# A filter table saved to DRAM in the order in which it is read back, and table work moved between engines

## The chip, the cores and the metric

The kernel runs on one core of one Trainium2 chip. The metric is the device time of one execution in microseconds (us). The core has a matrix engine (TensorE, PE; its weight loads are listed as PEld), VectorE (DVE), ScalarE (ACT), GpSimd (POOL) and an engine that only issues transfers (SyncE, SP). Each engine works through its own instructions in their order, and waits where one needs the result of another engine or of a transfer. Transfers issued by SP and by POOL are carried out by the same 16 DMA engines.

## The reference

The input x has 8 batches of 3008 rows and 256 channels. Along the rows it is filtered in the frequency domain, and then each row goes through a two-layer network with an exact GELU between the layers.

```python
X = np.fft.rfft(x, axis=1)                      # x: (8, 3008, 256)
F = (filt_r + 1j * filt_i)[None, :, :]          # filt_r, filt_i: (1505, 256)
y = np.fft.irfft(X * F, n=3008, axis=1)
x = y.reshape(8 * 3008, 256)
h = x @ w_in                                    # w_in: (256, 2048)
g = 0.5 * h * (1.0 + erf(h / sqrt(2)))
out = g @ w_out                                 # w_out: (2048, 256), out: (24064, 256)
```

## The kernel before

The row number is split as 3008 = 47 x 64, and so is the frequency. A transform is then two smaller ones, each a matrix product with a table of sines. Batch 0 is transformed in a head, before the network can start, by functions whose names begin with c. Batches 1 to 7 are transformed beside the network of the batch before them, in four steps s1 to s4. Between the steps the data is written to DRAM and read back in another order: R1 after s1, R2 after s3.

The network is a list of slots. A tile t has 512 rows of the output and 16 slots. In slot s = 16 t + j TensorE computes one 128-wide piece j of the first layer of tile t (mm1), on which ScalarE then does the GELU, and a sixteenth of the second layer of tile t - 1 (mm2, or mm2_seven). The transforms, tables and loads are hung on slots by put(slot, function, arguments); what is hung on a slot comes before the matrix products of that slot on each engine.

```python
for s in range((NT + 1) * 16):
    t, jc = s // 16, s % 16
    for f, a in at.pop(s, ()):
        f(*a)
    if t >= 1:
        (m.mm2_seven if t - 1 in seven else m.mm2)(t - 1, jc)
    if t < NT:
        m.mm1(t, jc)
```

mm1 writes to PSUM banks of kind h (three of them), the second layer to kind o (two), and the transforms mostly to kind f (three). mm2_seven does the second layer with seven products in place of eight (Strassen's scheme, for all tiles but the first and the last). It needs sums of pieces of the GELU's output, made on VectorE for each tile (sums_1, sums_2, sums_3, tiles s_sb and g_sb), and sums of pieces of w_out, made once (weight_sums, tile w_sums).

The filters lie in the tile F, with 128 rows. Rows 0 to 63 are loaded from the inputs: q = 0 is a frequency and q = 1 its mirror. In the head, rows 64 to 127 are a copy of rows 0 to 63. From batch 1 on the rows are wanted in another order, in which even and odd rows (the parity, par) stand apart. So F is saved to DRAM (Fd) and read back.

```python
def save_filters(self):
    self.Fd = self.dram.tile([64, 2, K1, 256], BF16, tag="Fd", name="Fd")
    self.nc.sync.dma_start(out=self.Fd, in_=self.F[0:64])

def load_filters_again(self, k0, k):
    for par in range(2):
        for r in range(2):
            for q in range(2):
                o = 64 * par + 32 * r + 16 * q
                self.nc.sync.dma_start(out=self.F[o:o + 16, :, k0:k0 + k, :],
                                       in_=self.Fd[32 * q + (par ^ q):32 * q + 32:2, :, k0:k0 + k, :])
```

K1 is 24. The second step, s2, multiplies by a table (T2p) and by F. Product p uses k = 2p and 2p + 1 of F:

```python
def s2(self, b, p):                             # p = 0 .. 11
    ps = self.bank("ps_s2")
    for i in range(2):
        k = 2 * p + i
        nc.tensor.matmul(ps[...], lhsT=self.T2p[:, k]..., rhs=self.st[b, "b", k // 6][:, k % 6, :], ...)
    w = self.st[b, "p", p] = self.pp.tile([128, 2, 512], BF16, tag="p12", name="p12")
    nc.vector.tensor_tensor(out=w, in0=ps.unsqueeze(1).to_broadcast([128, 2, 512]),
                            in1=self.F[:, :, 2 * p:2 * p + 2, :]..., op=ALU.mult)
```

Its other input, b_sb, is read from R1 by r1, in four pieces, and R1 is written by s1, in four groups c of four transfers. The tile a_sb between has three buffers, so that the fourth group waits for the writes of the first.

```python
def s1(self, b, c):
    a = self.pa.tile([128, 2, 4, 256], BF16, tag="a", name="a_sb")        # 3 buffers
    ps = [[self.bank("ps_s1", "h" if i == h == 0 else "f") for h in range(2)] for i in range(2)]
    ...                                                                   # 8 products
    for i in range(2):
        for h in range(2):
            self._evac(a[...], ps[i][h], "act" if h else False)           # ScalarE, or VectorE
    for r in range(2):
        for h in range(2):
            nc.sync.dma_start(out=o[:, w:w + 4, :], in_=a[64 * r:64 * r + 48, h])
```

Tables for batches 1 to 7 are made in the first slots: T2p (table_2_parities, GpSimd), U (table_u_pick on GpSimd, table_u on PE and ACT) and T4a (table_4_rows and weights_4 on GpSimd, table_4_factors on PE and ACT, and table_4_all, 24 operations on GpSimd). Loads of x and of the weights are issued by GpSimd, in its order.

```python
def weight_sums(self):
    w = self.w_out_sb.rearrange("p (i k) (n o) -> p k n i o", k=2, n=2)
    q, tt = self.w_sums, self.nc.gpsimd.tensor_tensor
    for o, a, b, op in ((q[:, 0], w[:, 0, 1], w[:, 0, 0], ALU.subtract), ...):    # four sums
        for i in range(0, 8, 2):
            tt(out=o[:, i:i + 2], in0=a[:, i:i + 2], in1=b[:, i:i + 2], op=op)
...
if b == 1:
    s1, n1, r1, s2, n2, group, r2, s4, n4 = 0, 4, 15, 25, 2.5, 12, 62, 70, 0.62
unit = lambda p: s2 + group * (p // 4) + int(n2 * (p % 4))    # the slot of product p
...
put(0, m.table_2_parities)
put(1, m.table_u_pick, g)
put(1, m.table_4_rows, g)
put(1, m.weights_4, g)
put(10, m.load_filters_again, 0, 8)
put(16, m.load_filters_again, 8, 16)
put(4, m.weight_sums)
put(12, m.table_4_factors, g)
put(14, m.table_u)
put(15, m.table_4_all, g)
```

The whole kernel:

Of the kernel before, what the change touches and what calls it, by code (L numbers as in the profile page):

```python
# [12 lines left out]
BF16 = mybir.dt.bfloat16  # L13
# [6 lines left out]
K1 = 24  # L20
# [10 lines left out]
class _Mix:  # L31
# [62 lines left out]
            for q, a in enumerate((direct, mirror)):  # L94
                nc.gpsimd.dma_start(out=self.F[32 * q:32 * q + 32, t, k0:k0 + k, :], in_=a)

    def save_filters(self):
        self.Fd = self.dram.tile([64, 2, K1, 256], BF16, tag="Fd", name="Fd")
        self.nc.sync.dma_start(out=self.Fd, in_=self.F[0:64])

    def load_filters_again(self, k0, k):

        for par in range(2):
            for r in range(2):
                for q in range(2):
                    o = 64 * par + 32 * r + 16 * q
                    self.nc.sync.dma_start(out=self.F[o:o + 16, :, k0:k0 + k, :],
                                           in_=self.Fd[32 * q + (par ^ q):32 * q + 32:2, :, k0:k0 + k, :])

    def dup_filters(self, eng, k0, k):  # L110
        for k in range(k0, k0 + k, 2):
# [263 lines left out]
    def s1(self, b, c):  # L375

        nc = self.nc
        if c == 0:
            self.st[b, "R1"] = self.dram.tile([NB, 48, 256], BF16, tag="R1", name="R1")
        a = self.pa.tile([128, 2, 4, 256], BF16, tag="a", name="a_sb")  # L380
        x = self.st[b, "x"]
# [4 lines that stand above are left out]
                    w = 8 * c + 4 * r + 2 * i  # L386
                    nc.tensor.matmul(ps[i][h][64 * r:64 * r + 64, :], lhsT=self.T1s[64 * h:64 * h + NA],  # L387
                                     rhs=x[64 * h:64 * h + NA, w:w + 2, :], start=True, stop=True)
        for i in range(2):
            for h in range(2):  # L390
                self._evac(a[:, h, 2 * i:2 * i + 2, :].rearrange("p a b -> p (a b)"), ps[i][h], "act" if h else False)
        o = self.st[b, "R1"].rearrange("n q c -> q n c")
        for r in range(2):
            for h in range(2):
                w = HB * h + 8 * c + 4 * r
                nc.sync.dma_start(out=o[:, w:w + 4, :], in_=a[64 * r:64 * r + 48, h])
# [209 lines left out]
    def weight_sums(self):  # L606

        w = self.w_out_sb.rearrange("p (i k) (n o) -> p k n i o", k=2, n=2)
        q, tt = self.w_sums, self.nc.gpsimd.tensor_tensor
        for o, a, b, op in ((q[:, 0], w[:, 0, 1], w[:, 0, 0], ALU.subtract), (q[:, 1], w[:, 1, 1], q[:, 0], ALU.add),  # L610
                            (q[:, 2], w[:, 1, 1], w[:, 0, 1], ALU.add), (q[:, 3], w[:, 1, 0], q[:, 1], ALU.subtract)):
            for i in range(0, 8, 2):
                tt(out=o[:, i:i + 2], in0=a[:, i:i + 2], in1=b[:, i:i + 2], op=op)

    def quarters(self, t):

# [77 lines left out]
def kernel(  # L694
# [9 lines left out]
    m = _Mix(ctx, tc, x, filt_r, filt_i, moe_w_in, moe_w_out, out)  # L704
# [4 lines left out]
    g = m.small  # L709
    wide = ctx.enter_context(ExitStack())  # L710
    m.psum(wide, w=(2, 1), m=(1, 1), n=(5, 1))
    act = "act"
# [30 lines left out]

    nc.gpsimd.memset(m.vt[:, :, 96, :], 0.0)
    m.dup_filters(nc.gpsimd, 4, 20)
    m.save_filters()


    m.table_2_sin(0)
# [31 lines left out]
    for q in range(1, 7):  # L781
        if q < 6:
            m.c2(2 * q)
            if q + 2 < 6:
                m.c1t(q + 2, (act,))
            if q != 3:
                m.warm_up(2)
            m.c2(2 * q + 1)
        if q < 6:
            m.c3(2 * q - 2)  # L790
            if q == 3:
                m.table_3(2)
                m.table_3_copy(2, True)
            else:
                m.warm_up(1)
        else:
            m.c3(10, 1)
            m.warm_up(1)
            m.c3(11, 1)
# [20 lines left out]
    def put(slot, f, *a):  # L820
        at.setdefault(slot, []).append((f, a))

    def first(b):
        return (b * S // TCH) * 16

    for b in range(1, B):
        hi = first(b)
        if b == 1:
            s1, n1, r1, s2, n2, group, r2, s4, n4 = 0, 4, 15, 25, 2.5, 12, 62, 70, 0.62
        else:  # L830
            s1, n1, r1, s2, n2, group, r2, s4, n4 = hi - 94, 3.7, hi - 80, hi - 71, 3.4, 14, hi - 25, hi - 17, 1
        unit = lambda p: s2 + group * (p // 4) + int(n2 * (p % 4))
        for u in range(16):
            put(s4 + int(u * n4), m.s4, b, u // 2, u % 2)
        for c in range(4):
            put(s1 + int(c * n1), m.s1, b, c)
            put(r1 if c < 3 else unit(3) + 1, m.r1, b, c)
            put(r2 if c < 3 else s4 + int(4 * n4) + 1, m.r2, b, c)
        for p in range(12):
            put(unit(p), m.s2, b, p)  # L840
            if p % 4 == 3:
                put(unit(p) + 3, m.s3, b, p // 4)
                put(unit(p) + 4, m.s3_out, b, p // 4, 1)
        if b + 1 < B:
            for i in range(8):
                put(unit(i + 2) if b > 1 else 25, m.load_next, b, i + 2, i // 2, i % 2)

    put(0, m.table_2_parities)
    put(1, m.table_u_pick, g)
    put(1, m.table_4_rows, g)  # L850
    put(1, m.weights_4, g)
    put(10, m.load_filters_again, 0, 8)
    put(16, m.load_filters_again, 8, 16)
    put(4, m.weight_sums)
    put(12, m.table_4_factors, g)
    put(14, m.table_u)
    put(15, m.table_4_all, g)
    seven = range(1, NT - 1)
    for t in seven:
        for i, s in enumerate((12, 13, 15, 17)):  # L860
# [4 lines left out]
    for s in range((NT + 1) * 16):  # L865
        t, jc = s // 16, s % 16
# [37 lines left out]
```

## Time and profile before

| what | value |
|---|---|
| time, median of 3 runs | 759.7 us (759.42 to 761.75) |
| span of the profiled execution | 758.5 us |
| TensorE busy | 741.2 us, 98% |
| VectorE busy | 581.4 us, 77% |
| ScalarE busy | 547.6 us, 72% |
| GpSimd busy | 111.6 us, 15% |
| reload of F, 8 transfers of 128 KB | 5.1 us from issue to landing (median) |
| reload of F, 8 transfers of 256 KB | 12.1 us from issue to landing (median) |

The page of a profile gives busy time by engine, the chain of work that ended last, and the costliest groups of instructions, named by the line of the kernel, the engine and the tiles as out<-in. A busy PE is not PE at its peak: products at half clock count as busy. Questions put to the trace give windows (the busy time of each engine in a stretch of time, its clock and what the DMA engines moved), waits (who waited for whom and how long) and a timeline. A wait for several things is put down to what came last by the profile, which is not always the true cause.

### The profile page before, as it was taken

Reading aid. Unit: us, or ns where it says so; the run is one execution under the profiler, and the core shown is the slowest. Engines: PE = TensorE matmul, PEld = TensorE weight load, DVE = VectorE, ACT = ScalarE, POOL = GpSimd, SP = SyncE. Lnnn points to the kernel's source line nnn. Section 1 sums busy time; section 2 is a strip of 40 time slices with the busy share of each in tenths; the row PEclk is TensorE's granted clock in tenths of the full one; section 3 lists DMA queues with packets and bytes.
Section 4 is the critical chain, followed back from the end, with each engine's and each line's share of the span. In section 5 each row is a group of like instructions: output and inputs, shape, how many; then the busy total and the mean of one; then the engine's idle time right before and its main releaser. Section 6 shows DMA issues by size and latency. Waiting matters only on the chain.

```text
span 758.5 us, 20181 instructions
## 1 busy us (share of the span) xinstructions
PE 741.2 (98%) x8388; PEld 519.3 (68%) x8388; DVE 581.4 (77%) x1043; ACT 547.6 (72%) x967; POOL 111.6 (15%) x207
## 2 busy tenths in 40 slices
PE   8988899999999999999999999999999999999998
PEld 4835567666777667666677666766677766777776
DVE  7935888799677986889777897779977799666562
ACT  7885567766787677867778667876678767777773
POOL 7969600021000210002000120001200000000000
PEclk9999999999999999999999999999999999999999
DMA  9999935555624745347525465254562432501011
GB/s 147 221 191 172 197 107 130 148 120 124 140 78 126 159 112 113 100 131 169 119 75 141 139 132 127 79 165 111 105 168 65 140 92 81 129 29 57 29 57 57
DMA packets 91500, 90.71 MB, mean 120 GB/s; under 512 B 7632, under 2 KB 78416, under 8 KB 91088
## 3 DMA queue, kind: packets, MB, share of 16 engines
q1 hardware_dynamic: 83024, 73.43, 36.2%
q0 software_dynamic: 8384, 16.00, 13.9%
q8 instruction: 65, 1.06, 0.6%
q14 instruction: 27, 0.22, 0.1%
HBM read 57.15 MB, written 48.23 MB: 139 GB/s over the span
## 4 chain that ended last, share of the span: by engine, by line
PE 85%; DVE 7%; DMA 4%; issue 1%; ACT 1%; POOL 0%; SPq 0%; DVEq 0%; ACTq 0%; POOLq 0%
PE ps_h L569 38%; PE ps_o L657 35%; PE ps_s L455 3%; PE ps_s L427 2%; DVE p L413 2%; DVE s_sb L627 2%; PE ps_s L410 2%; PE ps_s L387 2%; DMA b_sb<-R 2%; PE ps_o L596 1%; DMA R<-a_sb 1%; DMA x_sb<-in_x_dram 1%; PE ps_c L517 1%; ACT y_sb L295 1%; DVE ost L680 1%
## 5 line engine op out<-in xcount | busy, mean ns | idle before, releaser
L572 ACT ACTIVATE g_sb<-ps_h 128x512 f16<-128x512 f32 x752 | 448.2, 599 | 191.1 <-PE ps_h L569 188.7
L569 PE MATMUL ps_h<-y_sb,w_in_sb 128*128 128x512 bf16 (+3 forms) x1600 | 448.2, 368 | 1.3 <-ACT g_sb L572 0.8
L657 PEld LDWEIGHTS <-g_sb 128*128 128x128 f16 x2880 | 190.3, 98 | 81.7 <-issue 16.9
L657 PEld LDWEIGHTS <-s_sb 128*128 128x128 f16 x2160 | 147.3, 98 | 51.3 <-issue 3.3
L569 PEld LDWEIGHTS <-w_in_sb 128*128 128x128 bf16 x1600 | 125.2, 98 | 9.3 <-issue 3.6
L657 PE MATMUL ps_o<-w_sums,g_sb 128*128 128x128 f16 x1440 | 125.0, 219 | 2.2 <-DVE t_sb L673 1.5
L657 PE MATMUL ps_o<-w_sums,s_sb 128*128 128x128 f16 x1440 | 124.5, 219 | 0.0
L627 DVE TENSOR_TENSOR s_sb<-g_sb 128x1024 f16<-128x1024 f16 x180 | 121.4, 697 | 0.0
L413 DVE TENSOR_TENSOR p<-ps_s,F 128x1024 bf16<-128x1024 f32 x84 | 102.6, 1221 | 23.2 <-PE ps_s L410 15.8
L657 PE MATMUL ps_o<-w_out_sb,g_sb 128*128 128x128 f16 x1440 | 118.4, 219 | 0.4
L118 POOL COPY gate<-p 1x1 bf16<-1x1 bf16 x40 | 19.4, 484 | 415.3 <-DVE p L413 415.3
L633 DVE TENSOR_TENSOR g_sb<-s_sb,g_sb 128x1024 f16<-128x1024 f16 x90 | 62.3, 693 | 1.1
L657 PE MATMUL ps_o<-w_out_sb,s_sb 128*128 128x128 f16 x720 | 62.2, 219 | 0.0
L640 DVE TENSOR_TENSOR s_sb<-g_sb 128x1024 f16<-128x1024 f16 x90 | 61.5, 683 | 0.0
L299 DVE TENSOR_SCALAR y_sb<-ps_s 128x376 bf16<-128x376 f32 x56 | 30.6, 546 | 28.9 <-PE ps_s L455 28.9
L297 DVE CAST a_sb<-ps_s 128x512 bf16<-128x512 f32 x56 | 36.1, 686 | 18.6 <-PE ps_s L387 15.4
L455 PEld LDWEIGHTS <-d_sb 96*128 96x128 bf16 x448 | 31.2, 98 | 26.4 <-issue 1.9
L675 DVE TENSOR_TENSOR t_sb<-t_sb,ps_o 128x256 f32<-128x256 f32 x45 | 18.7, 416 | 38.5 <-PE ps_o L657 38.5
L672 DVE TENSOR_TENSOR ost<-t_sb,ps_o 128x256 f32<-128x256 f32 x45 | 18.9, 419 | 31.2 <-PE ps_o L657 31.2
L680 DVE TENSOR_TENSOR ost<-t_sb,ps_o 128x256 f32<-128x256 f32 x90 | 33.7, 416 | 6.8 <-PE ps_o L657 6.8
L455 PE MATMUL ps_s<-T4a,d_sb 96*128 96x94 bf16 x448 | 37.1, 206 | 1.0 <-DMA d_sb<-R 0.9
L410 PE MATMUL ps_s<-b_sb,T2p 128*128 128x256 bf16 x168 | 32.3, 274 | 2.1 <-DMA b_sb<-R 2.1
(149 smaller groups left out, 524.3 us busy)
## 6 DMA issues: line engine op xcount, KB each, us to landing
out_dram<-ost SPq DMA_DIRECT2D x93, 256.0 KB, 2.7
x_sb<-in_x_dram POOLq DMA_DIRECT2D x64, 188.0 KB, 3.6
R<-a_sb SPq DMA_DIRECT2D x112, 96.0 KB, 2.2
b_sb<-R SPq DMA_DIRECT2D x28, 384.0 KB, 4.4
R<-v_sb SPq DMA_DIRECT2D x84, 128.0 KB, 2.4
d_sb<-R SPq DMA_DIRECT2D x56, 192.0 KB, 3.9
F<-Fd SPq DMA_DIRECT2D x8, 256.0 KB, 12.1
Fd<-F SPq DMA_DIRECT2D x1, 1536.0 KB, 9.9
```

Source lines behind the costliest of these rows:

```text
L297: self.nc.vector.tensor_copy(out=out, in_=in_)
L299: self.nc.vector.tensor_scalar(out=out, in0=in_, scalar1=scale, scalar2=None, op0=ALU.mult)
L410: nc.tensor.matmul(ps[:, 256 * i:256 * i + 256], lhsT=self.T2p[:, k].rearrange("p a b c d -> p (a b c d)"), rhs=self.st[b, "b", k // 6][:, ...
L413: nc.vector.tensor_tensor(out=w, in0=ps.unsqueeze(1).to_broadcast([128, 2, 512]), in1=self.F[:, :, 2 * p:2 * p + 2, :].rearrange("p t a b ...
L455: nc.tensor.matmul(ps[:, 94 * i:94 * i + 94], lhsT=d[:, (grp % 2) * 4 + i, 128 * half:128 * half + 128], rhs=self.T4a[:, 4 * grp + i], sta ...
L569: nc.tensor.matmul(ps[:, o:o + n], lhsT=self.w_in_sb[:, dc, jc * 128:jc * 128 + 128], rhs=self.ring[:, dc, off:off + n], start=(dc == 0), ...
L572: nc.scalar.activation(out=self.st["g", t][:, jc, :], in_=ps, func=AF.Gelu)
L627: self.nc.vector.tensor_tensor(out=self.st["s", t][:, i:i + 2], in0=a, in1=b, op=ALU.subtract)
L633: self.nc.vector.tensor_tensor(out=a21[:, k], in0=self.st["s", t][:, k, 0], in1=a22[:, k], op=ALU.add)
L640: self.nc.vector.tensor_tensor(out=self.st["s4", t][:, k], in0=a12[:, k], in1=s2[:, k], op=ALU.subtract)
L657: nc.tensor.matmul(ps[:, (m + 1) % 2, sub, :], lhsT=a[:, i, 128 * sub:128 * sub + 128], rhs=b[:, i], start=i == 0, stop=i == 7)
L680: v(out=c(h, 1 - h), in0=tt, in1=p, op=ALU.add)
```

## The change

Its parts:

- The copy of the filters in DRAM is laid out in the order in which it is read back. It is written in two calls of four transfers each, and read back in transfers of 32 rows of one of the two filters, in place of 16 rows of both.
- The first third of it (k = 0 to 7) is read back in the head, before the transfers of R1, and not at slot 10. The rest stays near its slot (17 in place of 16).
- The sums of the weights are made by VectorE, in four operations, and not by GpSimd in 16, at slot 17 and not 4.
- In batch 1 one of the two evacuations of s1 on ScalarE goes to VectorE.
- The table work of batch 1 has other slots and another order on GpSimd, and s2, r2 and s4 of batch 1 begin three slots earlier, with s4 spread wider.

It is meant to have the inputs of batch 1 ready earlier, and to leave GpSimd free for the table T4a.

```diff
-    def save_filters(self):
-        self.Fd = self.dram.tile([64, 2, K1, 256], BF16, tag="Fd", name="Fd")
-        self.nc.sync.dma_start(out=self.Fd, in_=self.F[0:64])
+    def save_filters(self, k0, k):
+        if "Fd" not in self.st:
+            self.st["Fd"] = self.dram.tile([2, 2, 16, 2, K1, 256], BF16, tag="Fd", name="Fd")
+        for t in range(2):
+            for q in range(2):
+                o = self.st["Fd"][:, q, :, t, k0:k0 + k, :].rearrange("a i k c -> i a (k c)")
+                if q:
+                    o = o[:, ::-1]
+                self.nc.sync.dma_start(out=o, in_=self.F[32 * q:32 * q + 32, t, k0:k0 + k, :])
 
     def load_filters_again(self, k0, k):
-        for par in range(2):
-            for r in range(2):
-                for q in range(2):
-                    o = 64 * par + 32 * r + 16 * q
-                    self.nc.sync.dma_start(out=self.F[o:o + 16, :, k0:k0 + k, :],
-                                           in_=self.Fd[32 * q + (par ^ q):32 * q + 32:2, :, k0:k0 + k, :])
+        for t in range(2):
+            for o in range(0, 128, 32):
+                i = self.st["Fd"][o // 64, :, :, t, k0:k0 + k, :].rearrange("q i k c -> (q i) (k c)")
+                self.nc.sync.dma_start(out=self.F[o:o + 32, t, k0:k0 + k, :], in_=i)
@@ s1
-                self._evac(a[:, h, 2 * i:2 * i + 2, :]..., ps[i][h], "act" if h else False)
+                self._evac(a[:, h, 2 * i:2 * i + 2, :]..., ps[i][h], "act" if h and (b > 1 or i) else False)
@@ weight_sums
-        q, tt = self.w_sums, self.nc.gpsimd.tensor_tensor
+        q, tt = self.w_sums, self.nc.vector.tensor_tensor
-            for i in range(0, 8, 2):
-                tt(out=o[:, i:i + 2], in0=a[:, i:i + 2], in1=b[:, i:i + 2], op=op)
+            tt(out=o, in0=a, in1=b, op=op)
@@ the head
-    m.save_filters()
+    for k in (12, 0):
+        m.save_filters(k, 12)
@@ the head, q counts 1 to 6
             m.c3(2 * q - 2)
+            if q == 2:
+                m.load_filters_again(0, 8)
@@ batch 1
-            s1, n1, r1, s2, n2, group, r2, s4, n4 = 0, 4, 15, 25, 2.5, 12, 62, 70, 0.62
+            s1, n1, r1, s2, n2, group, r2, s4, n4 = 0, 4, 15, 22, 2.5, 12, 59, 67, 0.75
@@ the slots
+    put(0, m.table_4_rows, g)
+    put(0, m.weights_4, g)
+    put(0, m.table_u_pick, g)
     put(0, m.table_2_parities)
-    put(1, m.table_u_pick, g)
-    put(1, m.table_4_rows, g)
-    put(1, m.weights_4, g)
-    put(10, m.load_filters_again, 0, 8)
-    put(16, m.load_filters_again, 8, 16)
-    put(4, m.weight_sums)
-    put(12, m.table_4_factors, g)
-    put(14, m.table_u)
-    put(15, m.table_4_all, g)
+    put(7, m.table_4_factors, g)
+    put(11, m.table_u)
+    put(11, m.table_4_all, g)
+    put(17, m.load_filters_again, 8, 16)
+    put(17, m.weight_sums)
```

More of the change, by code (lines that the diff above doesn't have):

```diff
@@ L390, in s1 @@
             for h in range(2):
-                self._evac(a[:, h, 2 * i:2 * i + 2, :].rearrange("p a b -> p (a b)"), ps[i][h], "act" if h else False)
+                self._evac(a[:, h, 2 * i:2 * i + 2, :].rearrange("p a b -> p (a b)"), ps[i][h],
+                           "act" if h and (b > 1 or i) else False)
         o = self.st[b, "R1"].rearrange("n q c -> q n c")
```

## The prediction

> **What bounds the kernel now.** I read the page first, then the waits, then the windows, to find where the 758.5 us could give. The share of busy time on the page and its chain of waits say the same:
>
> ```profile
> PE 741.2 (98%) x8388; PEld 519.3 (68%) x8388; DVE 581.4 (77%) x1043; ACT 547.6 (72%) x967; POOL 111.6 (15%) x207
> ...
> PE 85%; DVE 7%; DMA 4%; issue 1%; ACT 1%; POOL 0%; SPq 0%; DVEq 0%; ACTq 0%; POOLq 0%
> ```
>
> TensorE sets the time over the span. From the third batch of work on nothing of this change is left to gain: the diff touches the head and batch 1 alone. So only the part before about 126 us counts, and there the windows of 2 us show where TensorE is idle or slow (columns: stretch, PE, PEld, DVE, ACT, POOL busy, granted clock, DMA share, GB/s):
>
> ```profile
> 48.00:50.00 2.00, 0.48 (x5) 0.33 (x5) 1.12 (x2) 1.09 (x2) 0.00 (x0) 1.00 0.79 207
> 50.00:52.00 2.00, 2.00 (x9) 0.82 (x7) 0.17 (x1) 1.96 (x7) 1.02 (x2) 0.66 0.71 193
> 52.00:54.00 2.00, 2.00 (x8) 1.06 (x7) 0.00 (x0) 1.01 (x2) 2.00 (x4) 0.50 1.10 182
> ...
> 62.00:64.00 2.00, 0.73 (x7) 0.66 (x8) 0.30 (x1) 0.00 (x0) 1.92 (x3) 1.00 1.03 404
> 64.00:66.00 2.00, 2.00 (x9) 1.04 (x8) 0.93 (x1) 0.60 (x1) 1.84 (x4) 0.57 1.17 256
> 66.00:68.00 2.00, 2.00 (x10) 1.16 (x9) 1.18 (x2) 0.60 (x1) 1.84 (x4) 0.58 1.03 135
> ...
> 70.00:72.00 2.00, 2.00 (x18) 1.42 (x16) 2.00 (x3) 1.24 (x3) 1.85 (x2) 1.00 1.02 131
> 72.00:74.00 2.00, 2.00 (x27) 1.53 (x26) 2.00 (x3) 1.33 (x3) 1.92 (x3) 1.00 1.02 131
> 74.00:76.00 2.00, 2.00 (x28) 0.93 (x26) 2.00 (x3) 1.54 (x3) 1.92 (x3) 1.00 1.02 131
> ...
> 84.00:86.00 2.00, 0.58 (x6) 0.45 (x7) 1.97 (x4) 0.38 (x1) 2.00 (x4) 1.00 0.49 84
> ```
>
> Three holes in PE (48 to 50, 62 to 64, 84 to 86); after each of the first two the clock falls to half for some 3.4 us; and VectorE is full from 68 on while the DMA rate stands at 131 GB/s. The waits of the same stretch name the causes (waiter, what it waited for: us in total, times, longest):
>
> ```profile
> DVE p L413 <- DMA out_dram<-ost: 3.4, 1, 3.4
> DVE p L413 <- DMA b_sb<-R: 3.1, 1, 3.1
> ...
> PE ps_s L410 <- DMA b_sb<-R: 2.1, 1, 2.1
> ...
> PE ps_o L657 <- DVE t_sb L673: 1.5, 1, 1.5
> ```
>
> and, in the stretch 39.9 to 60, `PE ps_t L351 <- ACT a_sb L295: 1.9`, itself behind the write of the first R group. The first row is not what it says: the output store only landed last. The product p12 needs rows of F; the last of the eight 256 KB filter transfers was issued at 65.7 us and took 16.5 us to land, that is at 82.2, and the product starts at 82.57.
>
> Slots (one mm1 each, told by the gelu on ACT) are my clock. Slot 0 starts at 39.9, slot 16 at 54.3, slot 24 at 61.2, slot 28 at 69.1, slot 40 at 81.9, slot 48 at 93.0, slot 80 at 125.8. From there batches of 94 slots take 88 to 89 us, 0.94 a slot. Slot 24 to 28 took 7.8 us instead of 3.8, and slot 40 to 48 took 11.1 instead of 7.5.
>
> **What the skill says.** "SBUF — State Buffer", Door 1 (the DMA port swizzle): a transfer's rate follows the SBUF ports its partitions reach; partitions 0..15 reach 4 ports, 0..31 reach 8, and it measures 104 and 189 GB/s. The trace agrees in kind: transfers of 16 rows run at a flat 131 GB/s with the DMA share at 1.02, and 404 GB/s stands at 62 to 64, where b_sb is read with 128 rows. The same page, on two separate sides: VectorE with two SBUF inputs and GpSimd take a shared port pair as a lock, and the loser blocks. The trace agrees: the sums s_sb<-g_sb have a median of 1308 ns between 60 and 80 us, beside GpSimd's table work, and 684 ns between 230 and 320. "TensorE: Matmul & The Clock Gate", Part 1: the clock falls to half after an idle window of about 3.4 us and comes back after a busy one. The trace shows two stretches of 3.41 us at 0.5, from 50.6 and 64.3, each just after a hole; that the hole was under 2.1 us does not quite fit the rule of a full idle window, so I do not count on losing one with a shorter hole.
>
> **The change, part by part.** The instruction order on PE is not longer; POOL loses 16 weight sums, VectorE gains 4 and four evacuations, ACT loses four.
>
> 1. Save and reload in parity order. The number and size of the reload transfers stay (8 of 128 KB, 8 of 256 KB); each covers 32 rows of one of the two filters instead of 16 rows of both. If the rate doubles to 260 GB/s, the eight large ones take 2 MB / 262 = 8 us instead of 16. They follow b_sb on the queue, which I put at 56 to 60 us, so they land near 68. The product that needs them is slot 34, reached at about 70. The wait of 3.4 us on VectorE and the 1.5 us of PE behind it go. Worth 3 us on the path.
>
> 2. First third in the head. The save is now 8 transfers of 192 KB, the first can go at 18.9 when its own filter rows have landed instead of 22.4. They and w_in end near 31 as before. The 1 MB of F comes at 29 to 35, where the window 30 to 32 has a DMA share of 0.58. It pushes the x and w_out loads by 1.5 to 2.5 us (w_out from 50.9 to about 53). In return the four last R writes no longer stand behind the F transfers on the same queue (issued 49.7 to 53.3; the R behind them 53.8 to 56.3, landed near 60). R should be whole near 55.5, b_sb in near 58.7 instead of 63.2. PE gets to the new slot 22 near 58. So the hole of 2.07 us shrinks to under 1, and the half clock behind it (3.41 us at 0.5, worth 1.7) goes. Worth 3 to 3.7 us.
>
> 3. Tables at other slots, one evacuation moved from ACT to VectorE. Slots 0 to 12 cost 2.86 us per four with ACT full (four gelus 2.1, two evacuations 1.1 overlapped). With one ACT evacuation less PE bounds them at about 2.4, so 1.3 us less by slot 12. But the fourth group needs a free a_sb, and the first R write lands at 48.5 as before (6.8 us for a transfer of 96 KB while w_out shares the DMA engines). PE runs slots 12 and 13 ahead of it, as the table matmuls no longer stand in front. The hole stays about 2 us, with its half clock, but 2 slots lie ahead of it. Worth 1.5 us.
>
> 4. Weight sums. 16 x 667 ns = 10.7 us leave GpSimd, so the 24 operations of the last table begin at about 47 and end near 69 instead of 59.7 and 84. On VectorE they are 4 operations of 0.68, or 1.3 beside GpSimd: 2.7 to 5.2 us, from w_out's landing (53) to at most 58.3, in a stretch where VectorE waited 9.8 us for nothing but the first output. They end just as the first product could start. What is won: of the seven-product sums some 5 operations lose their 0.6 us of lock, 3 us of VectorE, half of it on the path: 1.5 us.
>
> Against: w_out later by 2 us could stop PE at slot 18, which I put at 53.3 us: 0.5 to 1 lost. Sum: 3 + 3.4 + 1.5 + 1.5 - 0.8 = 8.6; as these overlap (a VectorE no longer late hides some of it), I take 7.7 us.
>
> **Rivals.** (a) w_out becomes the wait. The DMA engines are full from 34 to 50 us (share 1.0 to 1.3). If the 1 MB costs the loads its full 4 us, w_out lands at 55 and x too late for the s1 groups; PE stops at slot 18 and drops to half clock there. Then what part 2 wins is spent, and only 3 to 4 us remain: 756. For it speaks the DMA share; against it the slack at 30 to 32. (b) VectorE is the bound from slot 28 to 67 whatever comes first. Twelve slots hold four products of 1.22, two v_sb casts of 0.67 and 6.3 us of the seven-product work (its sums and output adds, 8.4 us in 16 slots): 12.5 us against 11.4 of PE. Then the removed waits are paid back as VectorE backlog, and the win is that of the three slots by which s2 now begins earlier: 755. VectorE full at 68 to 78 and 86 to 98 speaks for it; that it had the 3.4 us of idle time in between speaks against. (c) All holes go, including the one at 48, since PE never idles long enough to lose the clock: 5 us more, 746. The R write under w_out speaks against it.
>
> **Range and chances.** Middle: 759.7 - 7.7 = 752.0. Rival (c) gives the lower end, 746; a new stall that eats nearly all gives 758. The ceiling: slot 80 could not come before 110.5 even with no loss from slot 0 on (16 x 0.6, 16 x 0.9, 48 x 0.97 from 39.9), which is 15.3 us, just what 2% (744.5) would need, so that is most unlikely: 0.05. Slower by over 2% would need 15 us of new stalls: 0.02.
>
> **What would show it.** Reload transfers of 256 KB at 1 us each rather than 2, all landed before 70. No wait of p on a filter transfer. b_sb landed by 59 and no half clock near 64. The hole near 48 still there. Sums s_sb at 0.69 us from 70 on. Slot 80 near 118. The prediction is wrong if w_out lands after 54 and PE waits for it, if 32 rows are no faster than 16, or if VectorE is full with PE waiting on it all through slots 28 to 67.

## The result and the profile after

The changed kernel takes 752.4 us (median of 4 runs, 752.06 to 753.29), the kernel before 760.5 us in the runs beside it (759.42 to 761.75). The ratio is 0.9895, with a 95% interval of 0.9874 to 0.9915. The prediction said 752.0. The two profiled executions that are read below differ by 7.0 us (spans of 758.5 and 751.5).

The page of the kernel after, its rows of busy time, of the chain that ended last, and of the filter's transfers (KB each, median us from issue to landing):

```profile
PE 740.1 (98%) x8388; PEld 518.9 (69%) x8388; DVE 585.8 (78%) x1051; ACT 545.8 (73%) x963; POOL 100.8 (13%) x191
...
PE 84%; DMA 8%; DVE 4%; POOL 1%; issue 1%; ACT 1%; SPq 1%; DVEq 0%; POOLq 0%; ACTq 0%
...
F<-Fd SPq DMA_DIRECT2D x8, 256.0 KB, 8.3
Fd<-F SPq DMA_DIRECT2D x8, 192.0 KB, 7.7
```

TensorE is the bound over the span as before. The large reloads take 8.3 us in place of 12.1. GpSimd has 11 us less to do, which is the 16 weight sums. The windows of 2 us (same columns as in the prediction) show where the time came from, and what did not come:

```profile
48.00:50.00 2.00, 0.27 (x2) 0.00 (x0) 0.00 (x0) 0.00 (x0) 1.84 (x3) 1.00 1.31 215
50.00:52.00 2.00, 0.85 (x3) 0.30 (x3) 1.60 (x3) 1.57 (x3) 1.92 (x3) 0.52 1.30 230
52.00:54.00 2.00, 2.00 (x8) 0.98 (x7) 0.29 (x1) 1.19 (x2) 1.90 (x3) 0.50 1.03 243
62.00:64.00 2.00, 2.00 (x16) 1.41 (x15) 1.85 (x2) 1.24 (x3) 1.84 (x4) 1.00 1.02 229
64.00:66.00 2.00, 2.00 (x16) 1.41 (x15) 0.55 (x1) 1.29 (x3) 1.92 (x3) 1.00 1.05 229
66.00:68.00 2.00, 2.00 (x16) 1.37 (x15) 2.00 (x3) 1.19 (x2) 1.92 (x3) 1.00 1.03 225
72.00:74.00 2.00, 2.00 (x27) 1.50 (x24) 2.00 (x4) 1.77 (x4) 0.00 (x0) 1.00 1.07 248
84.00:86.00 2.00, 2.00 (x24) 1.42 (x21) 2.00 (x3) 1.71 (x4) 0.00 (x0) 1.00 0.59 135
```

From 62 us on PE is full and at full clock in every row shown; the holes at 62 to 64 and at 84 to 86 are gone. The DMA engines move 229 GB/s at the same share of 1.02 at which they moved 131. But the hole at 48 grew, and from within it on the clock is at half for 6.83 us (50.1 to 56.9) where it was 3.41. The waits between 39.9 and 60 us give its cause:

```profile
DVE a_sb L302 <- DMA R<-a_sb: 4.6, 1, 4.6
...
PE ps_h L575 <- DVE a_sb L302: 2.9, 1, 2.9
DVE w_sums L618 <- DMA w_out_sb<-in_moe_w_out_dram: 2.7, 1, 2.7
```

PE waits 2.9 us (it was 1.9) for an evacuation that needs a free a_sb, which the R writes give back: the first group of them landed at 46.6 to 50.3, before at 46.6 to 48.8. VectorE waits for w_out, which came at 54.9 in place of 50.9. Between 60 and 126 us no row with a product p behind a filter or an output transfer is left; what p still waits for is PE:

```profile
DVE p L419 <- PE ps_s L416: 2.8, 2, 1.6
...
PE ps_s L461 <- DMA d_sb<-R: 0.8, 1, 0.8
```

Read by slots (time of the slot's GELU in the profiled execution):

| slot | before | after | gained since the slot above |
|---|---|---|---|
| 0 | 39.9 | 39.5 | 0.4 |
| 12 | 50.6 | 50.9 | -0.7 |
| 24 | 61.2 | 63.5 | -2.0 |
| 48 | 93.0 | 87.5 | 7.8 |
| 80 | 125.8 | 119.1 | 1.2 |
| 188 | 228.3 | 221.6 | 0 |

At slot 24 the changed kernel is 2.3 us behind. All of its gain, and more, lies between slots 24 and 48, and nothing is gained after slot 80. The 0.4 us at slot 0 can't be counted as a gain: in the runs below it comes between 39.1 and 40.2 us whatever the head holds (42.2 in e10). The execution read here is also the slowest of its four (753.3 us): in e8 and e10, where all that is loaded up to slot 16 is the same, w_out lands at 53.5 and 53.0 (54.9 here) and b_sb at 59.0 and 59.3 (60.1 here). So about 1 us of what this trace shows ahead of slot 24 is its own.

### The profile page after: what moved, and what is told of

It reads as the page before. It is cut to its first block, busy times and chain, and to the rows that moved or that the text cites. A ratio compares the mean times of both kernels' runs of the same rounds, so it can differ in the third digit from the quotient of the medians.

```text
span 751.5 us, 20173 instructions
## 1 busy us (share of the span) xinstructions
PE 740.1 (98%) x8388; PEld 518.9 (69%) x8388; DVE 585.8 (78%) x1051; ACT 545.8 (73%) x963; POOL 100.8 (13%) x191
## 4 chain that ended last, share of the span: by engine, by line
PE 84%; DMA 8%; DVE 4%; POOL 1%; issue 1%; ACT 1%; SPq 1%; DVEq 0%; POOLq 0%; ACTq 0%
PE ps_h L575 38%; PE ps_o L662 34%; PE ps_s L433 3%; PE ps_s L461 3%; PE ps_s L416 2%; DMA R<-a_sb 2%; PE ps_o L602 2%; PE ps_s L392 2%; DVE p L419 2%; DMA F<-Fd 1%; DVE s_sb L632 1%; DMA Fd<-F 1%; DMA w_in_sb<-in_moe_w_in_dram 1%; DMA d_sb<-R 1%; DMA x_sb<-in_x_dram 1%; DMA R<-v_sb 1%
## 5 line engine op out<-in xcount | busy, mean ns | idle before, releaser
L632 DVE TENSOR_TENSOR s_sb<-g_sb 128x1024 f16<-128x1024 f16 x180 | 119.4, 686 | 0.0
L662 PE MATMUL ps_o<-w_out_sb,s_sb 128*128 128x128 f16 x720 | 62.2, 219 | 0.0
L645 DVE TENSOR_TENSOR s_sb<-g_sb 128x1024 f16<-128x1024 f16 x90 | 61.3, 681 | 0.0
L302 DVE CAST a_sb<-ps_s 128x512 bf16<-128x512 f32 x60 | 38.5, 685 | 18.6 <-PE ps_s L392 13.9
L86 POOL DMA_DIRECT2D x_sb<-in_x_dram x64 | 33.0, 520 | 2.5 <-issue 2.5
```

The source lines that it names most:

```text
L86: nc.gpsimd.dma_start(out=xt[h * o:h * o + NA, w:w + 8, :], in_=xv[h][:, w:w + 8, :])
L302: self.nc.vector.tensor_copy(out=out, in_=in_)
L632: self.nc.vector.tensor_tensor(out=self.st["s", t][:, i:i + 2], in0=a, in1=b, op=ALU.subtract)
L645: self.nc.vector.tensor_tensor(out=self.st["s4", t][:, k], in0=a12[:, k], in1=s2[:, k], op=ALU.subtract)
L662: nc.tensor.matmul(ps[:, (m + 1) % 2, sub, :], lhsT=a[:, i, 128 * sub:128 * sub + 128], rhs=b[:, i], start=i == 0, stop=i == 7)
```

## The experiments

The theory after this reading: the rows of the reload carry most of the gain; time up to slot 24 is set by the landing of b_sb, the data that step s2 reads, so what PE wins or loses ahead of it counts for nothing; and GpSimd without the weight sums spares VectorE. The main rival: the first third in the head is what brings b_sb early, and the stall at slot 12 still costs the slots it seems to cost. Every time below stands beside runs of the kernel before on the same chip (medians 760.6 to 761.5), so ratios are compared, with 95% intervals. The changed kernel's is 0.9895 [0.9874, 0.9915]. Diffs are against the changed kernel where nothing else is said.

### e2: the reload in 16 rows again

```diff
-        for t in range(2):
-            for o in range(0, 128, 32):
-                i = self.st["Fd"][o // 64, :, :, t, k0:k0 + k, :].rearrange("q i k c -> (q i) (k c)")
-                self.nc.sync.dma_start(out=self.F[o:o + 32, t, k0:k0 + k, :], in_=i)
+        for o in range(0, 128, 16):
+            self.nc.sync.dma_start(out=self.F[o:o + 16, :, k0:k0 + k, :],
+                                   in_=self.st["Fd"][o // 64, o // 16 % 2, :, :, k0:k0 + k, :])
```

> The changed kernel, but F is read back in transfers of 16 rows of both filters (same layout in DRAM, same number and size of transfers). Theory: 16 rows halve the rate of the reload; the eight large transfers land 2 us apart instead of 1.2, the last near 77 us instead of 71.9, the fifth product waits for it at about 72, and VectorE and PE lose 3 to 5 us: 755 to 757. Rival: VectorE is the bound in this stage and hides the wait: at most 1 us slower, 753.

Measured 762.9 us (22 runs, 760.0 to 766.9), ratio 1.0022 [1.0009, 1.0036]: the whole gain is lost and a little more, 9.7 us against the changed kernel (0.0127 of 761), about twice the most that was expected. Size and number of transfers and the layout in DRAM are the same and only the rows differ, yet the large ones land 2.1 us apart, the last at 82.05. So it is the rows, and not the layout, that the rate follows. Waits of e2 between 60 and 126 us:

```profile
DVE p L418 <- issue: 7.7, 1, 7.7
...
PE ps_o L661 <- DVE g_sb L637: 7.0, 1, 7.0
```

The row with "issue" has no releaser in the trace, but the product starts at 82.32, just after the landing. Behind it in VectorE's order stand the sums that PE needs, so PE stops for 7.0 us (77.2 to 84.2), and the clock is at half for 6.83 us (81.7 to 88.6). That is more than the same late landing cost the kernel before, where PE waited 1.5 us. A likely reason is that s2 now begins three slots earlier, so that this product stands at slot 34 in place of 37 and VectorE comes to it 4.5 us sooner (74.6 in place of 79.1); no run puts the old slots beside 16 rows, so this is not shown.

### e7: the rows of 32 alone

The kernel before with the parity layout and the transfers of 32 rows, and nothing else of the change (save in one call of four transfers, first third at slot 10, sums on GpSimd, old slots and evacuations).

> The kernel before, with the layout in parity order and the reload in transfers of 32 rows alone (at slots 10 and 16 as before, the save in one call of 4 transfers). Theory: with 16 rows the changed kernel gave back its whole gain, so the rows carry most of it: the 256 KB transfers land by about 71 instead of 82, the wait of the fifth product (3.4 us on VectorE, 1.5 on PE, and the backlog behind) goes, b_sb lands some 2 us earlier: 754 to 756.5. Rival: the gain needs the other parts too, since the fifth product comes at slot 37 here and VectorE is slowed by the last table until 84 us: 758 to 760.

Measured 754.0 us, ratio 0.9915 [0.9900, 0.9931]: 6.5 us of the gain (0.0085 of 761) come from this alone. The third read at slot 10 lands at 52.4 to 56.4 (before: 53.7 to 58.9), so b_sb, which follows it on the queue, lands at 60.7 in place of 63.2, and PE has no hole and no half clock there. The rest lands by 73.9 and no product waits for it. By the times of the slots e7 wins 3.6 us on the kernel before between slots 24 and 28, where the hole and the half clock go, and 2.8 us between slots 40 and 48, where the wait of the fifth product goes. The interval overlaps that of the whole change, so the other parts together bring about 1.5 us that the two runs don't separate. Windows of 4 us of e7:

```profile
70.00:74.00 4.00, 3.69 (x44) 2.02 (x41) 3.97 (x4) 2.76 (x6) 3.84 (x4) 1.00 0.92 277
74.00:78.00 4.00, 2.85 (x29) 2.00 (x30) 4.00 (x7) 1.40 (x3) 3.77 (x5) 1.00 0.30 75
```

and the same of the changed kernel:

```profile
70.00:74.00 4.00, 4.00 (x53) 2.66 (x54) 4.00 (x7) 2.98 (x6) 1.63 (x4) 1.00 1.02 275
74.00:78.00 4.00, 4.00 (x45) 2.89 (x43) 3.96 (x8) 2.77 (x5) 0.00 (x0) 1.00 1.07 229
```

VectorE is full in both. In e7 GpSimd is still at its table (3.8 of 4.0) and PE falls short; in the changed kernel GpSimd is done with it at 67.5 (the 1.63 are issues of loads) and PE is full.

### e4: the weight sums on GpSimd

```diff
+    put(4, m.weight_sums)
-    put(17, m.weight_sums)
```

and in weight_sums the 16 operations of before in place of four on VectorE.

> The changed kernel, but the weight sums are made by GpSimd at slot 4 in 16 operations, as before, ahead of the last table. Theory: the sums wait for w_out until 55 us on GpSimd and the last table runs from about 61 to 86 us, beside the sums of the seven products on VectorE, which take 1.3 instead of 0.68 us each; VectorE is full there, so 1.5 to 3 us slower: 754 to 755.5. Rival: what VectorE loses to the lock it wins back from the four weight sums, no difference: within 0.7 of the changed kernel.

Measured 756.2 us, ratio 0.9935 [0.9917, 0.9953], 3.0 us more than the changed kernel, the upper end of what was expected. Between 39.9 and 66 us the waits of e4 have this row at their head:

```profile
POOL w_sums L619 <- DMA w_out_sb<-in_moe_w_out_dram: 10.9, 2, 7.4
```

GpSimd waits 10.9 us for w_out and then has the sums to make, so its last table operation ends at 88.9 us and not at 67.5. VectorE pays beside it. The seven-product sums between 62 and 100 us, in e4:

```profile
L633 DVE TENSOR_TENSOR s_sb<-g_sb 128x1024 f16<-128x1024 f16 x8 | 8.4, 1062 | 0.0
```

and in the changed kernel:

```profile
L632 DVE TENSOR_TENSOR s_sb<-g_sb 128x1024 f16<-128x1024 f16 x11 | 8.0, 750 | 0.0
```

One operation takes 1062 ns on average in place of 750. "SBUF — State Buffer", section "Who interferes with whom", says that a VectorE operation with two inputs in SBUF, as these have, contends with a GpSimd operation that reads SBUF, since the port pair that they share is locked for one of them; this agrees in kind. Slots 24 to 80 take 58.9 us in e4 and 55.6 in the changed kernel. The run doesn't part the sums' own 10.7 us from the wait for w_out, which the third in the head has lengthened: in e7, where w_out comes at 48.1, GpSimd waits 3.7 us for it.

### e1: a buffer of its own for the fourth group

If the stall at slot 12 counts, removing its cause must bring its 2.9 us and the half clock.

```diff
-        a = self.pa.tile([128, 2, 4, 256], BF16, tag="a", name="a_sb")
+        pool, tag = (self.pd, "d") if b == 1 and c == 3 else (self.pa, "a")
+        a = pool.tile([128, 2, 4, 256], BF16, tag=tag, name="a_sb")
```

> The changed kernel, with a buffer of its own for the fourth group of s1 in batch 1 (taken from the d tiles, so that it does not wait for the first R writes). Theory: the hole of PE at 48 to 51 us, now 2.9 us with 6.8 us of half clock behind it, is the wait for a free a_sb; without it the hole and most of the half clock go, 4 to 6 us: about 747. Rival: the DMA engines are behind whatever waits first; then PE stops two slots further on, at slot 18, for the second half of w_out, which lands at 54.9 us, with half clock again: within 1.5 us of the changed kernel, 751 to 753.

Measured 753.0 us, ratio 0.9895 [0.9878, 0.9912]: no difference, the rival was right. The waits of e1 between 39.9 and 66 us:

```profile
DVE w_sums L619 <- DMA w_out_sb<-in_moe_w_out_dram: 5.2, 1, 5.2
...
PE ps_o L603 <- DMA w_out_sb<-in_moe_w_out_dram: 2.9, 1, 2.9
```

The same 2.9 us stand at slot 18, where PE needs w_out (landed at 53.7). The wait for w_out was there all along, hidden behind the wait for a_sb. Half clock follows here too (3.41 us, from 54.5). b_sb lands 0.9 us earlier and slot 24 comes 0.9 us earlier, which can't be put down to the buffer, since e8 and e10 have b_sb as early without it. The time is the same.

### e10: the evacuations as before

```diff
-                           "act" if h and (b > 1 or i) else False)
+                           "act" if h else False)
```

> The changed kernel, with two of four evacuations of s1 on ScalarE in batch 1, as before. Theory: slots 0 to 12 take 1.3 us longer, but the fourth group waits for the first R writes (50.3 us) anyway, so nothing is lost: within 0.7 us of the changed kernel. Rival, the prediction's own term: 1 to 1.5 us slower, 753.5 to 754.5.

Measured 753.5 us, ratio 0.9903 [0.9886, 0.9920]: 0.6 us more by the ratios, no difference that can be measured, though the rival's 1 us isn't excluded either. The profiled execution is useful by accident: its clock was full only from 10.7 us on, and slot 0 came at 42.2, 2.6 us late. Yet b_sb landed at 59.3 and slot 24 came at 62.7, 0.8 us before the changed kernel's. PE had caught up in front of a wait for transfers. In every kernel with s2 at slot 22 and the full clock there, slot 24 comes 3.38 us after the first b_sb has landed, to 0.01 us: 60.12 and 63.50 in the changed kernel, 59.22 and 62.59 in e1, 61.67 and 65.05 in e2, 59.58 and 62.96 in e4, 59.29 and 62.67 in e10, 58.23 and 61.61 in e12; e5, e6 and e9 below give the same.

### e3: the first third at slot 10

```diff
             m.c3(2 * q - 2)
-            if q == 2:
-                m.load_filters_again(0, 8)
@@
+    put(10, m.load_filters_again, 0, 8)
```

> The changed kernel, but the first third of F is read back at slot 10, as before, and not in the head. Theory from the trace of the changed kernel: in the head it delays x, w_out (54.9 instead of 50.9 us) and the first R writes (50.3 instead of 48.8), so the hole at 48 us is deeper than before; at slot 10 the hole shrinks to about 2 us with 3.4 us of half clock and b_sb lands near 61, so the whole is within 1 us of the changed kernel: 751.5 to 753.5. Rival, the prediction's own term: the place in the head was worth 3.4 us, so 755 to 756.

Measured 755.4 us, ratio 0.9921 [0.9907, 0.9936]: about 2.0 us more than the changed kernel, nearer to the rival; but the two intervals overlap, so the 2.0 us are not certain. The early part is better without the third in the head: w_out lands at 47.5, the first R writes at 46.3 to 47.9, PE waits 0.5 us for a_sb, and slot 20 comes at 54.2, 5.2 us ahead. But the last R writes stand behind the third on the queue, b_sb lands at 60.5 all the same, and PE now stops for it. Waits of e3 between 39.9 and 66 us:

```profile
PE ps_s L416 <- DMA b_sb<-R: 5.6, 1, 5.6
```

PE stands still for 5.6 us (55.0 to 60.6), the clock is at half for 6.83 us (59.7 to 66.6), and slot 24 comes at 66.8 (6.3 us after the landing in place of 3.4). So the head placement brings b_sb earlier by only 0.3 us against e3 in the trace of the changed kernel, and by 1.2 to 1.5 us in those of e10 and e8. It spreads the same wait over places that cost no clock behind b_sb.

### e12: no reload of the first third

```diff
-            if q == 2:
-                m.load_filters_again(0, 8)
```

This leaves out the reload of the first third (eight transfers, 1 MB): the first four products of batches 1 to 7 take the rows in the head's order. It measures what that reload costs at its place in the head.

> The changed kernel without the reload of the first third of F: 8 transfers, 1 MB, are left out altogether, so the first four products of batches 1 to 7 use the filter rows in the head's order. Everything else runs as it is. Theory: up to slot 24 the time is the sum of the transfers ahead of b_sb, wherever they stand; with 1 MB less, w_out lands near 47.5, R near 52, b_sb near 55.5, and slot 24 comes 4 to 5 us earlier than 63.5; the rest of F lands near 68 and nothing gives it back: 747 to 748.5. Rival: VectorE is the bound from slot 28 to 67, and it gives most back: 750.5 to 752.

Measured 750.7 us, ratio 0.9853 [0.9834, 0.9872]: 3.2 us less than the changed kernel, within the rival's range. R is whole at 54.9 and b_sb at 58.2, and PE waits 2.1 us for it. The first product of s2 on PE in e12 (start, us, what; in brackets the idle time before it and what ended it):

```profile
58.37 0.38 PE L416 MATMUL ps_s<-b_sb,T2p 128*128 128x256 bf16 x2 [2.06 <-DMA b_sb<-R]
```

and in the changed kernel:

```profile
60.26 0.38 PE L416 MATMUL ps_s<-b_sb,T2p 128*128 128x256 bf16 x2
```

The changed kernel's PE arrives just as b_sb does and shows no wait, which makes it look as if PE set the time; 0.14 us lie between landing and start in both. All that the third costs in the head is thus about 3 us by the medians, with intervals that barely part; the traces, counted from slot 0, give 2.5 us at slot 24 and 2.0 at slot 80. With the rest as it is, that bounds what another place for it could win.

### e5 and e6: the third behind b_sb

In e5 the third is read at slot 17 behind R and b_sb; e6 has the buffer of e1 as well.

```diff
-            if q == 2:
-                m.load_filters_again(0, 8)
@@
+    put(17, m.load_filters_again, 0, 8)
     put(17, m.load_filters_again, 8, 16)
```

> The changed kernel, but the first third of F is read back at slot 17, behind the R writes and the loads of b_sb, and not in the head. Theory: what sets the time up to slot 22 is the sum of transfers that lie ahead of b_sb; without the 1 MB of F ahead of them w_out lands near 47.5 and R near 52, b_sb near 55.5, the first third of F near 58; no hole of more than 1 us and no half clock, slot 24 near 58 instead of 63.5: 747 to 748.5. Rival: the wait moves to the first products, which need F, and to the rest of F, which comes 3 us later than the fifth product wants it; then most is lost again: 751 to 753.

> As e5_third_after_b, with the buffer of its own for the fourth group of s1. Theory: with w_out out of the way the first R writes land at 47.9, and the wait for a free a_sb costs PE only some 0.5 us, so the buffer brings at most 1 us over e5. Rival: the fourth R writes, issued 2 us earlier, bring b_sb earlier by as much, and 2 us more are won.

Measured 755.3 us, 0.9920 [0.9905, 0.9934], and 753.6 us, 0.9906 [0.9892, 0.9920]: the theory of e5 failed. There b_sb comes at 58.2 and not near 55.5. In e6 it comes 2.7 us earlier, as the rival of e6 had it, but only 1.1 us of time follow, with overlapping intervals. Everything up to b_sb is as hoped in e6 (R whole at 52.2, b_sb at 55.5, slot 24 at 58.9, 4.6 us before the changed kernel's), and then the first product waits for the third. Waits of e6 between 60 and 126 us:

```profile
DVE p L420 <- DMA F<-Fd: 9.4, 1, 9.4
```

In e6 the product starts at 62.9 where in the changed kernel the first one starts at 60.7, and slot 80 comes at 119.6 in place of 119.1. The wait has only changed its name.

### e9 and e11: both in the order in which they are needed

From e6, and with the diff against it: the first b_sb, the first third, the other two b_sb, the second third, the last third. e11 is e9 with s2, r2 and s4 at the slots of before.

```diff
-            put(r1 if c < 3 else unit(3) + 1, m.r1, b, c)
+            put((17 if b == 1 and c else r1) if c < 3 else unit(3) + 1, m.r1, b, c)
@@
-    put(17, m.load_filters_again, 0, 8)
-    put(17, m.load_filters_again, 8, 16)
+    put(16, m.load_filters_again, 0, 8)
+    put(17, m.load_filters_again, 8, 8)
+    put(17, m.load_filters_again, 16, 8)
```

> As e6_third_after_b_fourth, with the reads in the order in which they are needed: the first piece of b_sb, the first third of F, the other two pieces of b_sb, the second third of F, the last third. Theory: what e5 and e6 lost was the wait of the first product for F until 62.6 us, because three pieces of b_sb stood ahead of it; now F is there at about 59.5 and the fifth product's third at about 67: slot 32 near 67 instead of 70.4, 749.5 to 751. Rival: it is the sum of transfers again, b_sb's second piece and the later thirds come as much later; no better than e6, 752.5 to 754.

> As e9_b_and_f_in_turn, with the old slots of s2, r2 and s4 in batch 1 (25, 62, 70 with 0.62). Theory: PE meets s2 some 2.6 us later, when b_sb has landed (55.5), so the hole of 1.8 us in front of the first product goes and the wait for F is hidden; VectorE's crowding costs nothing, as in e8: 747.5 to 749.5, the best of all. Rival: with three slots fewer between s2 and the end of batch 1, s4 is squeezed and it is no better than e9.

Measured 754.7 us, 0.9913 [0.9899, 0.9928], and 754.0 us, 0.9905 [0.9891, 0.9919]: the rivals were right. The first third lands at 61.5 (e9) and 61.3 (e11), not at 59.5, and the first product still waits for it. Waits of e11 between 39.9 and 126 us:

```profile
DVE p L420 <- DMA F<-Fd: 4.7, 1, 4.7
```

What stands behind it on the queue comes later too: in e9 the last third lands at 76.6 and the fourth piece of b_sb at 82.4, where the changed kernel has them at 71.9 and 74.8. e11 has slot 24 at 57.3, 6.2 us before the changed kernel's, and slot 80 at 119.9, 0.8 us after it.

### e8: s2, r2 and s4 at the slots of before

```diff
-            s1, n1, r1, s2, n2, group, r2, s4, n4 = 0, 4, 15, 22, 2.5, 12, 59, 67, 0.75
+            s1, n1, r1, s2, n2, group, r2, s4, n4 = 0, 4, 15, 25, 2.5, 12, 62, 70, 0.62
```

> The changed kernel with the old slots of s2, r2 and s4 in batch 1 (25, 62, 70 with 0.62 instead of 22, 59, 67 with 0.75). Theory: b_sb lands at 60.1 when PE is at slot 22, so at slot 25 nothing waits for it, and the products fall three slots deeper into the stretch where VectorE also makes the sums of the seven products; s4 is packed tighter: 1 to 2 us slower, 753.5 to 754.5. Rival: the three slots are only a fit to b_sb and are worth nothing: within 0.7 us of the changed kernel.

Measured 752.6 us, ratio 0.9896 [0.9880, 0.9912]: the three slots make no measurable difference. Here b_sb lands at 59.0 and the first product of s2 starts at 62.2 on PE, without a wait. So with these slots the landing of b_sb doesn't set the time, and nothing is lost by it; what sets it from there on was not isolated. No kernel with all of the work in it beat the changed one; e1, e8 and e10 are as fast.

## Why the prediction was right, and where its terms were not

The time was right within 0.4 us (8.1 us gained, 7.7 predicted), and that close in part by luck. The mechanism was right in the parts that carry it, while the terms of the sum were mis-sized in both directions.

**1. Rows of 32 (3 us).** Right in kind, and the most mis-sized term: alone it brought 6.5 us (e7), and taken out of the whole it cost 9.7 (e2). The rate was a little lower than worked out: 229 GB/s and not 262, transfers about 1.2 us apart and not 1, the last landed at 71.9 and not by 70. "SBUF — State Buffer", Door 1, gives about 109 and 218 GB/s as what single transfers over partitions 0..15 and 0..31 tend to; a chain of transfers over changing rows ran at 131 and 229 here, above both, and the measured factor is 1.75 and not 2. What the term left out: the same faster transfers stand in front of b_sb. With them alone b_sb lands at 60.7, and the hole and half clock near 64 go (3.6 us of e7's gain). The prediction gave that to part 2. The wait of the fifth product, which the term was about, was worth 2.8 us in e7, as said.

**2. The third in the head (3 to 3.7 us).** The hole at 62 to 64 and the half clock behind it went as said, but they go with the rows alone (e7), where b_sb lands at 60.7. In the trace of the changed kernel w_out landed at 54.9 and not 53, R was whole at 56.7 and not 55.5, and b_sb landed at 60.1 and not 58.7; in e8, with the same head, these are 53.5, 55.5 and 59.0. So the landings were about right, and what they were worth was not. Undone alone (e3) the part costs about 2.0 us, which is not certain. The 1 MB of reload costs some 3 us in the head (e12), which the "slack" at 30 to 32 us did not hide, and none of the other places that were tried came out cheaper.

**3. Tables at other slots and one evacuation (1.5 us).** This step failed. In the first four slots the evacuation does what was said (2.41 us in place of 2.86). But the table products now stand at slot 7, and slot 11, the last one before the stall, comes 7.16 us after slot 0 where it came 7.17 us after it before, and not 1.3 less (7.83 in e10, without the evacuation). Slot 12 came 0.3 us later; the hole at 48 grew to 2.9 us and its half clock to 6.83. Evacuations (e10) and slots (e8) made no measurable difference each. e1 and e3 show where such a gain goes: what PE wins ahead of b_sb it waits away, at w_out (2.9 us in e1) or at b_sb itself (5.6 us in e3).

**4. Weight sums (1.5 us).** The operations cost what was worked out (0.69 to 1.46 us, 4.7 in sum, predicted 2.7 to 5.2), though w_out let them end at 59.5 only. From 70 to 110 us s_sb takes 680 ns on average, as said. The gain was mis-sized: 3.0 us in e4. There GpSimd also waits 10.9 us for w_out, which the term left out.

**Against: w_out (0.8 us).** It landed at 54.9, past the 54 that was named as a sign against the prediction (at 53.0 to 54.4 in e1, e4, e8 and e10, which have the same head), but PE stopped for a_sb first and reached slot 18 no sooner than w_out did.

**The sum.** The terms over-counted what comes before slot 24 (2.3 us were lost there in the trace, not won) and under-counted slots 24 to 80, which took 55.6 us in place of 64.6. Slot 80 was put near 118 and came at 119.1; it is 60.1 for b_sb, 3.4 to slot 24, and 55.6. That the two errors cancel to within 0.4 us of the time is luck.

**Rivals.** (a) w_out as the wait: half true. It is as late as that rival says, and would be the next stall (e1), but having it 7.3 us earlier won nothing in e3, where b_sb landed at 60.5 all the same. (b) VectorE as the bound: it is full from 66 to 78 us, but PE is full as well. With GpSimd still at its table PE does wait for VectorE's sums, 1.0 us in e7 and 1.6 in e4. (c) All holes go: no, the one at 48 stayed, and the wait for the R writes behind it is the reason that the prediction named.

## What to carry to other kernels

Where a chain of transfers feeds a stage, look for all the landings that its first instructions wait for (here b_sb, and with it the first third of F), and count only what moves the last of them: here work saved on an engine ahead of it was waited away (e1, e10), and moving a transfer out of the way of one landing handed the wait to the next thing on the queue (e5, e6, e9). A transfer over twice the rows of SBUF at the same size went 1.75 times as fast here, and all that queued behind it gained too. Undo a part alone and do it alone before giving it a share of a gain: here the rows were worth 6.5 us alone and 9.7 as the last part to be added.

## What the runs showed of the hardware

The clock does not follow the length of a hole by itself. The changed kernel and e4 have the same hole of 2.9 us at 48 us. Windows of 4 us behind it, in the changed kernel (half clock):

```profile
50.00:54.00 4.00, 2.85 (x9) 1.28 (x9) 1.89 (x3) 2.77 (x5) 3.82 (x5) 0.51 1.16 236
```

and in e4 (full clock):

```profile
50.00:54.00 4.00, 2.76 (x16) 1.56 (x16) 1.89 (x3) 3.51 (x7) 0.97 (x2) 1.00 0.84 201
```

Likewise a hole of 2.06 us in e12 cost no clock, and one of 2.07 us in the kernel before cost 3.41 us of half clock. From slot 0 to the last product half clock came only in stretches of 3.41 or 6.83 us, and the stretches at full clock ahead of them and between them are whole multiples of 3.41 too (44.37 is 13 of them, 23.89 in e2 is 7). So in each trace the clock changes on a grid of 3.41 us. Here is the step of the grid just ahead of the half clock in the changed kernel:

```profile
46.69:50.10 3.41, 1.58 (x12) 0.51 (x7) 0.00 (x0) 0.64 (x2) 3.18 (x5) 1.00 1.32 214
```

and the two steps over which the hole of e4 is spread:

```profile
45.95:49.36 3.41, 1.96 (x12) 0.65 (x13) 0.00 (x0) 1.08 (x3) 0.00 (x0) 1.00 1.32 218
49.36:52.77 3.41, 1.93 (x12) 1.16 (x12) 1.89 (x3) 2.55 (x5) 1.29 (x2) 1.00 0.94 214
```

PE is busy for 1.58 us of the one and for 1.96 and 1.93 us of the others. Laid over all fourteen traces up to 745 us, the grid has ten steps at full clock with PE busy for 47% or less, and half clock follows each of them; of the others, with 48% or more, it follows one (56%, in e8). Half clock lasted one step more where PE was busy for 27 to 72% of its first step, and ended after every step with 95% or more. So it seems to be the share of a step that decides, and a wholly idle step was not needed; this is a fit to traces that were taken for other questions. "TensorE: Matmul & The Clock Gate", Part 1, says that the activity window, of about 3.4 us, runs freely; the multiples of 3.41 and the two outcomes for one hole agree with that, and no run here tried to shift the window.

While w_out and the rest of x were loaded by the other queue, the first four 96 KB writes of R took 5.9 to 7.6 us from issue to landing; the last four, after those loads, landed 0.28 us apart. That the load of w_out holds them up is read from this order in time alone; a kernel with that load elsewhere was not tried.
